# Ten ssm_k blocks in the head with their writes behind the gathers, four logit products of a chunk together, list columns on GpSimd

## The chip, the cores and the metric

One core of one Trainium2 chip runs the whole program in one launch. The metric is device time in microseconds (us): the median of several executions of the program. One more execution was taken by the hardware profiler, and everything said of engines, waits and transfers comes from it.

## What is computed

The reference mixes two branches over 2048 tokens of 512 channels with a gate per token:

```python
x = A_q
g = _sigmoid((x * gate_w).sum(-1, keepdims=True))
a = _A_ref(x, A_k, A_v, A_shift_k, A_ssm_k, A_ssm_D)   # short conv of k, times v, long causal conv with ssm_k, times q
b = _B_ref(x, B_w_router, B_w_gate, B_w_up, B_w_down)  # top 2 of 8 experts: silu(x Wg) * (x Wu) Wd
return g * a + (1 - g) * b
```

`_A_ref` convolves 2048 steps per channel by FFT; `ssm_k` is its kernel. `_B_ref` routes each token to the two experts with the highest logits. Everything is float32, and the kernel keeps that accuracy: a product of the experts is three products of rounded parts (high by high, high by low, low by high).

## The kernel before

**The two branches.** The long convolution is done as a transform in two stages by matrix products. Stage 1 takes 16 blocks of `ssm_k` (here "ks blocks", `k_out` and `stage1_f32`, lines 276 to 314): a block of 128 x 512 is loaded (`kr`), two products with a constant matrix `c1` give 2 x 128 x 512 results, they are copied out of PSUM (`out1`) and written to a scratch `kd` in HBM. 16 blocks of the other input follow (`x_stage1`), then stage 2, the inverse, and `y_stage`. These steps are generators in a list `fill` (line 430), and `tick()` puts one more of them between the tiles of the experts. The experts run one after the other (`expert(r)`, lines 503 to 672): expert `r` has eleven tiles `ft` of the hidden width, with `up(ft)` (products `g` and `u` in two halves of the rows) and a `down` for each group of tiles. So TensorE has one long stream: products of the experts with a ks block, or a step of the other kind, between them now and then.

**The head.** Before the first expert can run, its rows must be known. The head (lines 694 to 934) is written in the order in which each engine is to run it, and kept so (`manual_schedule`); after it the framework orders the rest. It goes like this:

- SyncE loads the transposed input `qT` as 16 tiles `xt` of 128 x 512, four for each of four chunks of 512 tokens, then the constants and the first ks blocks.
- For each chunk (lines 772 to 780), four logit products (line 777) fill four groups of 32 partitions of one PSUM tile. `turn` transposes what an earlier chunk gave, between the second and the third product of the next one, and `ranks` (lines 760 to 767) makes masks of the top two on VectorE, five operations on 128 x 256 per chunk.
- A scan over the masks (line 791) and two pairs of small products (lines 794, 795) count and place the tokens. `key` (line 806) holds the counts; the expert with the most tokens becomes expert 0, its number goes into `eor0` for SyncE and ScalarE, and its rows are listed: `hots` (line 894) is a table of 128 x 16 x 128 zeros and ones in four operations, `vals` its columns (lines 881, 882), the list comes out of 16 products (line 897), and `gidx` (line 869) holds the row numbers.
- Five indirect DMAs on GpSimd (line 460) gather the rows of expert 0. Each gathered tile of 128 rows is transposed on TensorE (line 469, tile `xgp`), and copied out twice: ScalarE writes the rounded part `xh` (line 471), VectorE the rest `xl` (line 472). The first product of expert 0 (`product`, line 555, `hi_first`) takes four steps with `xh`, four with the low part of the weights, then four with `xl` of the first two tiles. `raw` is a tile of gate and up weights, split by ScalarE into `gh` and by VectorE into `gl`.
- Six ks blocks (`SEQ_N`) run in the head. Their results are written to `kd` by SyncE as each copy is done, the sixth by ScalarE after the gathers (`later`). `busy` puts products without a use into gaps of TensorE.

**Buffers.** A ks block's two copies go into two tiles with the tag "A" (six buffers) or one double tile with the tag "ev" (three buffers, `EV`, line 42). The loads `kr` use double tiles with the tag "B" (five). A new tile of a tag takes the buffer of the oldest, and whoever writes it waits until that one was read.

Of the kernel before, what the change touches and what calls it, by code (L numbers as in the profile page):

```python
# [21 lines left out]
P = 128  # L22
# [27 lines left out]
XT = 16  # L50
# [6 lines left out]
SEQ_N = 6  # L57
BUSY = (14, 3, 4, 1, 10, 6, 6)
# [77 lines left out]
def gated_mix(ctx: ExitStack, tc: tile.TileContext, a, out):  # L136
# [113 lines left out]
    def out1(p, dst, pl, name, later=False):  # L250
# [25 lines left out]
    def stage1_f32(x, dst, pl, name, later=False):  # L276
        if ordered and pl % 2 == 0:
            p = [turned(f"{name}p{t}") for t in range(2)]
# [11 lines left out]
        out1(p if ordered else both, dst, pl, name, later)  # L290
# [22 lines left out]
    def k_out(pl, later=False):  # L313
        stage1_f32(kr[pl], kd, pl, f"ks{pl}", later)
# [138 lines left out]
    def load_rows(r, n):  # L453
        w = min(P, CAPS[r] - n * P)
        col = r * TILES + n
        if r == 0 and n >= XG:
            xg = t2k("A", 6, f"xg{r}_{n}")
# [37 lines left out]
    def ticks(n):  # L495
        for _ in range(n):
            tick()

# [4 lines left out]
    def expert(r):  # L503
# [12 lines left out]
        def load(ft, eng=sync):  # L516
            fw = FT[ft][1]
            raw = wp.tile([P, 2 * KT * P], F32, tag="raw", bufs=R3[0], name=f"raw{r}_{ft}")
            n = 2 * KT * fw
            src = a["wgu"][ds(st["e"], 1), GU_OFF[ft]:GU_OFF[ft] + P * n].rearrange("o (p n) -> (o p) n", p=P)  # L520
            if r == 0 and ft in QN and not ordered:
                with after("act 0"):
                    act.dma_start(raw[:, :n], src)
# [4 lines left out]
            st["raw", ft] = raw[:, :n]  # L528

# [13 lines left out]
        def product(ft, h, u, hi_first=False):  # L543
# [13 lines left out]
            for kt in range(KT):  # L557
                last = mm3(p[:fw, :nn], ghv[:, u, kt], glv[:, u, kt], xh[:, kt, sl], xl[:, kt, sl],
                           start=(kt == 0), stop=(kt == KT - 1))
            return last  # L560

        def load_down(ft, eng=sync):
            f0, fw = FT[ft]
            rd = wp.tile([P, D], F32, tag="rd", bufs=R3[3], name=f"rd{r}_{ft}")
            src = a["wd"][ds(st["e"], 1), f0:f0 + fw, :].rearrange("o f d -> (o f) d")
            if r == 0 and ft in QR and not ordered:
                with after("act 0"):
                    act.dma_start(rd[:fw], src)
# [124 lines left out]

    first = expert(0)
# [4 lines left out]
    gt = rp.tile([P, PL * D // S, E, E], F32, name="gt")  # L699
    run = rp.tile([P, E + 1, PL], BF16, name="run")  # L700
    dve.memset(run[:, 0], 0.0)
    NB = S // D
    sums = rp.tile([P, 4, P], BF16, name="sums")
    pool.memset(sums[:, 2], 1.0)
    pool.memset(sums[:, 3], -1.0)
    xts = []
    for c in range(NB):
        for kt in range(KT):
            xts.append(rp.tile([P, D], F32, tag="xt", bufs=XT, name=f"xt{c}_{kt}"))
            anchor["sp"] = sync.dma_start(xts[-1], a["qT"][c, kt]).ins  # L710
        if c == 0:
            sync.dma_start(ident, a["c_small"][:, :P])
# [16 lines left out]
    def keep(c):  # L729
        lgT.append(rp.tile([P, D], F32, tag="lgT", bufs=4, name=f"lgT{c}"))  # L730
        act.activation(lgT[c], lgp[c], AF.Copy)
# [12 lines left out]
    CP = PL // NB  # L744
# [15 lines left out]
    def ranks(c):  # L760
        part = slice(c * CP, c * CP + CP)
        s4 = [P, CP, E, E]
        dve.tensor_reduce(L9[:, part], lt[c].rearrange("p (a k e) -> p a e k", a=CP, k=KT)[:, :, :E + 1], op=ALU.add, axis=AX.X)
        dve.tensor_tensor(gt, L[:, part].unsqueeze(2).to_broadcast(s4), L[:, part].unsqueeze(3).to_broadcast(s4), op=ALU.subtract)
        dve.tensor_tensor(gt, gt, tie.unsqueeze(1).to_broadcast(s4), op=ALU.is_ge)
        dve.tensor_reduce(rank[:, part], gt, op=ALU.add, axis=AX.X)
# [5 lines left out]
    for c in range(NB):  # L772
        for kt in range(KT):
            if c and kt == 2:
                turn(c - 1)
                ranks(c - 1)
            pe.matmul(lgp[c][32 * kt:32 * kt + 32], wk[:, kt], xts[c * KT + kt], start=True, stop=True)
# [4 lines left out]
    turn(NB - 1)  # L782
    ranks(NB - 1)
# [3 lines left out]
    k_out(k_order[0])  # L787
    k_load(k_order[5])
    k_out(k_order[1])
# [7 lines left out]
    k_out(k_order[2])  # L797
    k_out(k_order[3])
# [14 lines left out]
    dve.tensor_tensor(oh0, key, top.to_broadcast([P, E]), op=ALU.is_equal)  # L813
    s0 = rp.tile([P, PL], F32, name="s0")
    n0 = rp.tile([P, PL], F32, name="n0")
    u0 = rp.tile([P, PL], F32, name="u0")
    e0 = rp.tile([P, E], F32, name="e0")
    ef0 = rp.tile([P, 1], F32, name="ef0")
    g5 = rp.tile([P, PL, TILES], F32, name="g5")
    dve.tensor_mul(w0, w0, oh0.unsqueeze(2).to_broadcast([P, E, PL]))  # L820
    dve.tensor_mul(e0, oh0, io8)
    dve.tensor_reduce(s0, w0.rearrange("p e a -> p a e"), op=ALU.add, axis=AX.X)
    dve.tensor_reduce(ef0, e0, op=ALU.add, axis=AX.X)
    s5 = [P, PL, TILES]
# [6 lines left out]
    dve.tensor_tensor(g5, n0.unsqueeze(2).to_broadcast(s5), cols1[:, :TILES].unsqueeze(1).to_broadcast(s5), op=ALU.is_equal)  # L831

# [48 lines left out]
    dve.tensor_scalar(val0[:, :, 1], g5, own, None, op0=ALU.mult)  # L881
    dve.tensor_mul(val0[:, :, 0], g5, tok_hi.unsqueeze(2).to_broadcast(s5))
# [6 lines left out]
    k_out(k_order[4])  # L889
    act.activation(G, L9[:, :, E], AF.Exp, scale=-1.0)  # L890
    first.split(0, act)
    busy(none, BUSY[2])
    for i in range(0, PL, 4):
        dve.tensor_tensor(hot[:, i:i + 4], u0[:, i:i + 4].unsqueeze(2).to_broadcast([P, 4, P]),
                          io128n.unsqueeze(1).to_broadcast([P, 4, P]), op=ALU.is_equal)
        for j in range(i, i + 4):
            pe.matmul(pv0, hot[:, j], val0[:, j], start=(j == 0), stop=(j == PL - 1))
        if i + 4 < PL:
            busy(none, BUSY[3])
    read(0, pv0)  # L900
    k_out(k_order[5], later=True)
# [7 lines left out]
    act.activation(z, z, AF.Exp)  # L909
    rows0 = gather(0)  # L910
    next(rows0)
    busy(none, BUSY[4])
    next(rows0)
    first.split(0, dve, halves=(0,))
    busy(none, BUSY[5])
    next(rows0)
    first.split(0, dve, halves=(1,))
    for f in written:
        f()
    first.load(2, act)  # L920
    first.load_down(0, act)
    act.activation(sg0, key[:, :1], AF.Silu)
    busy(none, BUSY[6])
    first.product(0, 0, 0, hi_first=True)
    next(rows0)
    first.split(1, act)
    anchor["pe"] = first.product(0, 0, 1).ins
# [3 lines left out]
    ordered = False  # L931
    for _ in rows0:
        pass
    ticks(2)
# [234 lines left out]
```

## Time and profile before

| | |
|---|---|
| median of 3 runs | 965.4 us (963.39 to 966.9) |
| the profiled execution: its time | 962.82 us |
| its span | 960.9 us |
| TensorE (PE) busy | 941.3 us, 98% |
| VectorE (DVE), ScalarE (ACT), GpSimd (POOL) busy | 64%, 56%, 15% |
| granted TensorE clock, mean | 0.993 |

A profile is read from what TensorE waits for: with 98% of the span busy, only its few idle stretches and the work in its stream can give time back. A timeline row is one instruction, or several of a kind in a row, with its start, its busy time and, in brackets, the idle time ahead of it with what ended that. Consecutive products overlap, so what one costs in a full stream is the distance between starts.

### The profile page before, as it was taken

How to read it: one execution, taken by the hardware profiler on the slowest of the kernel's cores; microseconds unless marked ns; L12 is line 12 of the kernel's file. 1: busy time of each engine (PE TensorE's matmuls, PEld its weight loads, DVE VectorE, ACT ScalarE, POOL GpSimd, SP SyncE). 2: the span in 40 equal slices, each digit the busy share in tenths (PEclk: the TensorE clock that was granted, in tenths of full speed). 3: DMA queues.
4: the chain of work that ended last, by engine and by line, in shares of the span. 5: the costliest groups of instructions: out<-in, count | busy, mean ns of one | idle time of the engine just before them, and what ended most of it. 6: DMA issues, size and time to landing. Idle time of an engine off the chain costs nothing. (4 is left out here: it accounts for less than half of the span.)

```text
span 960.9 us, 18311 instructions
## 1 busy us (share of the span) xinstructions
PE 941.3 (98%) x7079; PEld 832.4 (87%) x7079; DVE 619.4 (64%) x1160; ACT 538.2 (56%) x881; POOL 139.6 (15%) x125
## 2 busy tenths in 40 slices
PE   8799999999999999999999999999999999999996
PEld 3589999999999999888889898888888887888895
DVE  4597689889999454745656555664676655554541
ACT  3453344454646645678667877677776672334330
POOL 1202011300103020031100301003120301020002
PEclk9899999999999999999999999999999999999998
DMA  8875875644657445474434754457453849875413
GB/s 299 308 265 195 302 244 179 174 149 168 220 179 197 145 135 187 146 183 167 143 129 161 179 170 152 128 169 182 164 165 113 207 143 315 268 197 143 116 31 44
DMA packets 78827, 171.93 MB, mean 179 GB/s; under 512 B 8625, under 2 KB 9521, under 8 KB 78610
## 3 DMA queue, kind: packets, MB, share of 16 engines
q1 hardware_dynamic: 55330, 122.57, 38.7%
q0 software_dynamic: 10976, 23.78, 12.1%
q10 hardware_dynamic: 12432, 24.38, 6.8%
q8 instruction: 57, 0.93, 0.4%
q14 instruction: 32, 0.26, 0.1%
HBM read 127.13 MB, written 43.57 MB: 178 GB/s over the span
## 5 line engine op out<-in xcount | busy, mean ns | idle before, releaser
L197 PE MATMUL g<-xh,gh 128*128 128x256 f32 (+15 forms) x700 | 202.7, 290 | 1.0 <-DVE sg L589 1.0
L197 PE MATMUL u<-xh,gh 128*128 128x256 f32 (+14 forms) x704 | 202.0, 287 | 0.7 <-ACT sg L588 0.6
L198 PE MATMUL u<-xl,gh 128*128 128x256 f32 (+14 forms) x704 | 201.6, 286 | 0.0
L199 PE MATMUL u<-xh,gl 128*128 128x256 f32 (+14 forms) x704 | 201.3, 286 | 0.0
L198 PE MATMUL g<-xl,gh 128*128 128x256 f32 (+15 forms) x700 | 200.1, 286 | 0.0
L199 PE MATMUL g<-xh,gl 128*128 128x256 f32 (+15 forms) x700 | 200.1, 286 | 0.0
L197 PEld LDWEIGHTS g<-xh,gh 128*128 128x128 f32 (+1 forms) x700 | 130.2, 186 | 16.9 <-issue 9.6
L197 PEld LDWEIGHTS u<-xh,gh 128*128 128x128 f32 (+1 forms) x704 | 130.9, 186 | 7.4 <-issue 4.0
L589 DVE TENSOR_TENSOR sg<-sg,u 128x256 f32<-128x256 f32 (+14 forms) x176 | 74.7, 425 | 95.8 <-PE u L199 84.9
L199 PEld LDWEIGHTS u<-xh,gl 128*128 128x128 f32 (+1 forms) x704 | 131.0, 186 | 5.7 <-issue 5.7
L590 ACT ACTIVATE hh<-sg 128x256 fp32r<-128x256 f32 (+14 forms) x176 | 73.5, 419 | 111.2 <-DVE sg L589 110.9
L198 PEld LDWEIGHTS u<-xl,gh 128*128 128x128 f32 (+1 forms) x704 | 131.0, 186 | 5.3 <-issue 4.9
L199 PEld LDWEIGHTS g<-xh,gl 128*128 128x128 f32 (+1 forms) x700 | 130.3, 186 | 5.9 <-issue 5.7
L198 PEld LDWEIGHTS g<-xl,gh 128*128 128x128 f32 (+1 forms) x700 | 130.2, 186 | 5.0 <-issue 3.2
L197 PE MATMUL yp<-hh,dh 128*128 128x264 f32 (+12 forms) x440 | 127.2, 291 | 0.0
L198 PE MATMUL yp<-hl,dh 128*128 128x264 f32 (+12 forms) x440 | 126.6, 289 | 0.0
L199 PE MATMUL yp<-hh,dl 128*128 128x264 f32 (+12 forms) x440 | 126.4, 289 | 0.0
L541 DVE TENSOR_TENSOR gl<-raw,gh 128x1024 fp32r<-128x1024 f32 (+2 forms) x89 | 105.4, 1184 | 22.9 <-ACT gh L535 22.2
L535 ACT ACTIVATE gh<-raw 128x1024 fp32r<-128x1024 f32 (+1 forms) x88 | 91.2, 1036 | 42.4 <-PE u L198 31.1
L588 ACT ACTIVATE sg<-g 128x256 f32<-128x256 f32 (+14 forms) x176 | 67.4, 386 | 80.8 <-PE g L199 72.2
L597 ACT ACTIVATE dh<-rd 128x512 fp32r<-128x512 f32 (+1 forms) x88 | 53.3, 627 | 70.5 <-DMA rd<-in_wd 30.6
L460 POOL DMA_INDIRECT xg<-in_q,gidx x37 | 44.7, 1207 | 325.8 <-PE xgp L469 288.7
(286 smaller groups left out, 1614.3 us busy)
## 6 DMA issues: line engine op xcount, KB each, us to landing
raw<-in_wgu SPq DMA_DIRECT2D x78, 512.0 KB
rd<-in_wd SPq DMA_DIRECT2D x77, 256.0 KB
kl<-kd SPq DMA_DIRECT2D x16, 512.0 KB
xl<-xd SPq DMA_DIRECT2D x32, 256.0 KB
zd<-ze ACTq DMA_DIRECT2D x16, 512.0 KB
zl<-zd SPq DMA_DIRECT2D x16, 512.0 KB
out<-zt SPq DMA_DIRECT2D x21, 256.0 KB
krow<-in_kpad SPq DMA_DIRECT2D x19, 256.0 KB
```

What stands on the lines that cost most here:

```text
L197: pe.matmul(p, wh, hi, start=start, stop=False)
L198: pe.matmul(p, wh, lo, start=False, stop=False)
L199: return pe.matmul(p, wl, hi, start=False, stop=stop)
L460: anchor["pool"] = pool.indirect_dma_start(out=xg[:w], out_offset=None, in_=a["q"], in_offset=bass.IndirectOffsetOnAxis(ap=gidx[:w, col:co ...
L535: act.activation(st["gh", ft], raw, AF.Copy)
L541: dve.tensor_sub(st["gl", ft][:, c], raw[:, c], st["gh", ft][:, c].bitcast(F32))
L588: act.activation(sg[:fw, :nn], pp[0][:fw, :nn], AF.Silu)
L589: dve.tensor_mul(sg[:fw, :nn], sg[:fw, :nn], pp[1][:fw, :nn])
L590: act.activation(hh[:fw, sl], sg[:fw, :nn], AF.Copy)
L597: act.activation(dh[:fw], rd[:fw], AF.Copy)
```

## The change

- **Logits.** The fifth entry of `NCH` splits the last chunk into two halves of 256 tokens; each half comes in one DMA whose rows are 256 elements long. The four logit products of a chunk stand together, and `turn` and `ranks` of the chunk before come ahead of them.
- **ks blocks.** Ten of them (`SEQ_N`) run in the head; all ten are loaded ahead of the expert's weights. All their writes to `kd` become `later`, that is, they are issued by GpSimd behind the gathers. Blocks 7, 8 and 10 are copied out by VectorE, 9 by ScalarE, 7 and 9 into "B" tiles, all other even ones into "ev" tiles. The two `tick()` at the end of the head are gone, and `c2` is loaded later.
- **The list.** `e0`, its sum and `eor0` move from VectorE to GpSimd, and so do the two list columns; the comparison that gave `g5` becomes a difference of neighbours in a wider comparison (`g6`). `hots` is made from `u0` and a table `io4`, both bf16, with four neighbours innermost, and its four operations feed 16 products that stand without `busy` between them. `xg` tiles 3 and 4 use "xt" buffers, of which there are now 12.
- **Counts.** `BUSY` has new numbers.

```diff
-XT = 16
+XT = 12
-SEQ_N = 6
-BUSY = (14, 3, 4, 1, 10, 6, 6)
+SEQ_N = 10
+BUSY = (14, 3, 1, 6, 3)
...
-        if pl % 2:
+        both = None
+        if home == "A":
             evs = [t2k("A", 6, f"{name}e{t}") for t in range(2)]
         else:
-            both = two("ev", f"{name}e")
+            both = two(home, f"{name}e")
             evs = [half(both, t) for t in range(2)]
         for t in range(2):
-            act.activation(evs[t], p[t], AF.Copy)
-            if later:
-                written.append(lambda t=t: act.dma_start(dst[:, t, pl, :], evs[t]))
+            if eng is dve:
+                dve.tensor_copy(evs[t], p[t])
             else:
+                act.activation(evs[t], p[t], AF.Copy)
+            if not later:
                 sync.dma_start(dst[:, t, pl, :], evs[t])
+        if later and both is not None:
+            written.append(lambda: pool.dma_start(dst[:, :, pl, :], split2(both)))
+        elif later:
+            written.extend(lambda t=t: pool.dma_start(dst[:, t, pl, :], evs[t]) for t in range(2))
...
+NCH = (4, 4, 4, 2, 2)
...
+            x2 = rp.tile([P, KT, n], F32, tag="x2", bufs=2, name=f"xt{c}")
+            anchor["sp"] = sync.dma_start(x2, a["qT"][b].rearrange("k p d -> p k d")[:, :, o:o + n]).ins
...
     for c in range(NB):
         for kt in range(KT):
-            if c and kt == 2:
-                turn(c - 1)
-                ranks(c - 1)
...
         busy(lgp[-1], BUSY[1])
+        turn(c)
+        ranks(c)
...
+    pool.tensor_mul(e0, oh0, io8)
...
+    for h in (4, 2, 1):
+        pool.tensor_add(e0[:, :h], e0[:, :h], e0[:, h:2 * h])
+    pool.tensor_copy(eor0, e0[:, :1])
...
+    pool.tensor_sub(g5, g6[:, :, :TILES], g6[:, :, 1:])
...
-    dve.tensor_scalar(val0[:, :, 1], g5, own, None, op0=ALU.mult)
-    dve.tensor_mul(val0[:, :, 0], g5, tok_hi.unsqueeze(2).to_broadcast(s5))
+    pool.tensor_mul(val0[:, :, 1], g5, own.unsqueeze(2).to_broadcast(s5))
+    pool.tensor_mul(val0[:, :, 0], g5, tok_hi.unsqueeze(2).to_broadcast(s5))
...
+    hot0 = hots[:, :PL * P].rearrange("p (i c j) -> p i c j", i=4, j=4)
+    for i in range(4):
+        dve.tensor_tensor(hot0[:, i], u0[:, 4 * i:4 * i + 4].unsqueeze(1).to_broadcast([P, P, 4]), io4, op=ALU.is_equal)
+        for j in range(4):
+            n = 4 * i + j
+            pe.matmul(pv0, hot0[:, i, :, j], val0[:, n], start=(n == 0), stop=(n == PL - 1))
...
     rows0 = gather(0)
     next(rows0)
+    k_out(k_order[6], home="B", eng=dve, later=True)
+    first.split(0, dve, halves=(0, 1))
+    evict = k_out(k_order[7], home="ev", banks_of=bank, eng=dve, later=True, hold=True)
+    busy(none, BUSY[3])
+    next(rows0)
+    evict()
+    evict = k_out(k_order[8], home="B", later=True, hold=True)
     busy(none, BUSY[4])
     next(rows0)
...
+    evict()
+    evict = k_out(k_order[9], home="ev", banks_of=turned, eng=dve, later=True, hold=True)
+    first.product(0, 0, 0, hi_first=True)
+    first.split(1, act)
+    evict()
     next(rows0)
-    first.split(0, dve, halves=(1,))
+    first.load(2, act)
+    first.load_down(0, act)
     for f in written:
         f()
...
-    ticks(2)
```

Three places of the order that comes out. First VectorE (DVE) around the first gathered tiles; `waits` names the kinds of semaphore an instruction waits on (`DMASW` ones are counted up by DMAs that GpSimd issued, `DMAHW` ones by those of SyncE and ScalarE). Before:

```order
L472 TENSOR_TENSOR xl_407<-xgp_0_428,xh_406 128x4x128 [waits Activation_49]
L541 TENSOR_TENSOR gl_0_435<-raw_0_346,gh_0_360 128x512 [waits DMAHW6_49]
L472 TENSOR_TENSOR xl_407<-xgp_1_443,xh_406 128x4x128 [waits Activation_49]
L541 TENSOR_TENSOR gl_0_435<-raw_0_346,gh_0_360 128x512
L472 TENSOR_TENSOR xl_407<-xgp_2_477,xh_406 128x4x128 [waits Activation_49]
L541 TENSOR_TENSOR gl_1_599<-raw_1_348,gh_1_484 128x1024 [waits DMAHW7_49,Activation_49]
```

and now, from the low part of the first weights on:

```order
L545 TENSOR_TENSOR gl_0_430<-raw_0_359,gh_0_402 128x1024 [waits DMAHW0_49,Activation_49]
L479 TENSOR_TENSOR xl_413<-xgp_0_442,xh_412 128x4x128 [waits Activation_49]
L264 COPY ks8e<-ks8p_432 128x512 [waits DMASW0_49]
L264 COPY ks8e<-ks8p_433 128x512
L479 TENSOR_TENSOR xl_413<-xgp_1_458,xh_412 128x4x128 [waits Activation_49]
L545 TENSOR_TENSOR gl_1_626<-raw_1_361,gh_1_485 128x1024 [waits DMAHW1_49,Activation_49]
L264 COPY ks10e<-ks10p_468 128x512 [waits DMASW3_49,PE_49]
L264 COPY ks10e<-ks10p_469 128x512
L479 TENSOR_TENSOR xl_413<-xgp_2_490,xh_412 128x4x128 [waits Activation_49]
```

The copies of blocks 8 and 10 now stand ahead of `xl` of tiles 1 and 2, and each waits on a DMA of GpSimd. Block 8 takes the buffer "ev" that block 2 had, and block 10 that of block 4, since only three are there (blocks 2, 4, 6, 8, 10 use them in turn); so the two waits are for the writes of blocks 2 and 4 to `kd`.

Second GpSimd (POOL), from the gathers of expert 0 on. Before:

```order
L460 DMA xg_0_408<-in_q,gidx 128x512 [waits DVE_49]
L460 DMA xg_1_410<-in_q,gidx 128x512
L460 DMA xg_2_412<-in_q,gidx 128x512
L460 DMA xg_3_414<-in_q,gidx 128x512 [waits DMAHW5_49,Activation_49]
L460 DMA xg_4_416<-in_q,gidx 56x512 [waits DMAHW6_49,Activation_49]
L311 TENSOR_TENSOR kr_1681<-kr_1681,dD 1x512 [waits DMAHW4_49,DMAHW2_49,DMAHW7_49,DMAHW1_49,PE_49]
```

and now:

```order
L467 DMA xg_0_414<-in_q,gidx 128x512 [waits DVE_49]
L467 DMA xg_1_416<-in_q,gidx 128x512
L467 DMA xg_2_418<-in_q,gidx 128x512
L467 DMA xg_3_420<-in_q,gidx 128x512 [waits PE_49]
L467 DMA xg_4_422<-in_q,gidx 56x512 [waits DMAHW2_49,PE_49]
L272 DMA kd<-ks1e_285 128x512 [waits Activation_49]
L272 DMA kd<-ks1e_286 128x512 [waits Activation_49]
L270 DMA kd<-ks2e 256x1x512 [waits DMASW0_49,Activation_49]
L272 DMA kd<-ks3e_305 128x512 [waits DMASW1_49,Activation_49]
```

All writes of the ten blocks now stand behind the gathers: the four shown here, then nine more, in the order of the blocks from the other half of 3 to 10. A block that went into two "A" tiles (1, 3, 5) has two writes of 128 rows, another one write of 256 rows. The write of block 2 waits on `DMASW0`, a count that gathers raise.

Third TensorE (PE), from the second gathered tile to the third, now (before, six `busy` products stood between `xgp_1` and the first `g`):

```order
L476 MATMUL xgp_1_458<-ident,xg_1_416 128x128 x4
L292 MATMUL ks10p_469<-kr_155,c_90 128x512
L292 MATMUL ks10p_468<-kr_155,c_90 128x512
L559 MATMUL g_0_0_472<-xh_412,gh_0_402 128x256 x4
L559 MATMUL g_0_0_472<-xh_412,gl_0_430 128x256 x4
L559 MATMUL g_0_0_472<-xl_413,gh_0_402 128x256 x4
L476 MATMUL xgp_2_490<-ident,xg_2_418 128x128 x4
```

The third run of `g`, with `xl`, is the one that needs the VectorE rows above; what is behind it waits with it.

## Rows read from the trace of the kernel before

**Rows 1.** The page, part 1: busy time, share of the span and instructions of each engine.

```profile
PE 941.3 (98%) x7079; PEld 832.4 (87%) x7079; DVE 619.4 (64%) x1160; ACT 538.2 (56%) x881; POOL 139.6 (15%) x125
```

**Rows 2.** The waits of TensorE's queue (PE) over the whole span, the longest: engine, line, tile, what it waited for, us in total, times, longest.

```profile
PE xgp L469 <- DMA xg<-in_q,gidx: 5.7, 1, 5.7
```

**Rows 3.** The timeline of PE from 16 to 45 us: start in us, busy us, engine, line, operation, out<-in, shapes, count, and in brackets the idle time before and what ended it.

```profile
16.00 1.05 PE L777 MATMUL lgp<-xt,wr 128*32 128x512 f32 x4
...
19.32 1.02 PE L286 MATMUL ks2p<-kr,c 64*128 64x512 f32 x4
...
35.00 1.08 PE L469 MATMUL xgp<-ident,xg 128*128 128x128 f32 x4 [5.66 <-DMA xg<-in_q,gidx]
...
39.15 0.90 PE L555 MATMUL g<-xh,gh 128*128 128x256 f32 x4
...
40.37 0.64 PE L555 MATMUL g<-xl,gh 128*128 128x256 f32 x4
...
40.84 0.60 PE L469 MATMUL xgp<-ident,xg 128*128 128x128 f32 x4
...
43.49 1.13 PE L286 MATMUL ks7p<-kr,c 64*128 64x512 f32 x4
...
44.55 0.41 PE L197 MATMUL g<-xh,gh 128*128 128x312 f32 x1
```

**Rows 4.** The same view of PE around one ssm_k block in the stream of products (ks8, block 8).

```profile
49.45 0.30 PE L199 MATMUL u<-xh,gl 128*128 128x312 f32 x1
...
49.69 1.13 PE L286 MATMUL ks8p<-kr,c 64*128 64x512 f32 x4
...
50.97 0.28 PE L198 MATMUL u<-xl,gh 128*128 128x256 f32 x1
```

**Rows 5.** The timeline of VectorE (DVE) from 16 to 39 us, same columns.

```profile
16.45 0.59 DVE L764 TENSOR_TENSOR gt<-L 128x256 f32<-128x256 f32 x1
...
18.46 0.31 DVE L763 TENSOR_REDUCE L<-lt 128x36 f32<-128x144 f32 x1 [0.18 <-PE lt L757]
...
18.81 0.42 DVE L764 TENSOR_TENSOR gt<-L 128x256 f32<-128x256 f32 x1
...
20.41 0.42 DVE L791 TENSOR_TENSOR_SCAN run<-ones,mask 128x128 bf16<-128x128 f32 x1
...
21.18 0.17 DVE L806 SCALAR_TENSOR_TENSOR key<-cn_ps,rc 128x8 f32<-128x8 f32 x1 [0.34 <-PE cn_ps L795]
...
22.18 0.16 DVE L821 TENSOR_TENSOR e<-oh,rc 128x8 f32<-128x8 f32 x1
...
22.30 0.37 DVE L822 TENSOR_REDUCE s<-w 128x16 f32<-128x128 f32 x1
...
23.34 0.23 DVE L831 TENSOR_TENSOR g<-n,rc 128x80 f32<-128x80 f32 x1
...
23.94 2.49 DVE L894 TENSOR_TENSOR hots<-u,rc 128x512 bf16<-128x512 f32 x4
...
27.18 0.17 DVE L869 TENSOR_SCALAR gidx<-idf 128x5 int32<-128x5 f32 x1
...
38.88 0.69 DVE L472 TENSOR_TENSOR xl<-xgp,xh 128x512 fp32r<-128x512 f32 x1 [0.84 <-ACT xh L471]
```

**Rows 6.** Groups of DVE's instructions over the whole span, shapes kept apart, columns as in the group view: line, engine, operation, out<-in, shapes, count, busy us, mean ns of one, idle us before them. These multiply two bf16 tables, the second (`pay`) repeated along the innermost axis.

```profile
L850 DVE TENSOR_TENSOR vals<-hots,pay 128x448 bf16<-128x448 bf16 x20 | 12.4, 663 | 0.0
...
L850 DVE TENSOR_TENSOR vals<-hots,pay 128x160 bf16<-128x160 bf16 x3 | 0.9, 338 | 0.0
```

**Rows 7.** The timeline of GpSimd (POOL) from 15 to 34 us, same columns: the first two rows are small operations, the last two the first and the last of the five gathers of expert 0.

```profile
15.92 0.29 POOL L784 CAST sums<-before 128x128 bf16<-128x128 f32 x1 [13.85 <-DMA before<-in_c_small]
...
16.30 0.45 POOL L785 TENSOR_TENSOR before<-before,ident 128x128 f32<-128x128 f32 x1
...
27.63 1.06 POOL L460 DMA_INDIRECT xg<-in_q,gidx  x1 [10.31 <-DVE gidx L869]
...
32.78 0.93 POOL L460 DMA_INDIRECT xg<-in_q,gidx  x1 [0.30 <-issue]
```

**Rows 8.** Groups of POOL's instructions over the whole span: line, engine, operation, out<-in, count, busy us, mean ns of one, idle us before them. `mi` is 128 rows, `ye` to `out` 256 rows of 2 KB.

```profile
L295 POOL DMA_DIRECT2D mi<-in_c_mi x16 | 10.0, 626 | 93.9 <-PE zp L368 68.8 <-PE u L199 14.3 <-PE u L198 10.7
...
L427 POOL DMA_DIRECT2D out<-ye x8 | 9.8, 1225 | 109.5 <-DVE ye L425 103.8 <-DMA out<-ya,sidx 5.7
```

**Rows 9.** Stretches of the span: us from:to, busy us of PE, PEld, DVE, ACT and POOL with instruction counts, granted TensorE clock (1.00 is 2.4 GHz, 0.50 is 1.2 GHz), DMA share, GB/s.

```profile
11.00:12.00 1.00, 1.00 (x9) 0.35 (x7) 0.93 (x3) 0.60 (x1) 0.00 (x0) 1.00 1.05 389
...
14.00:15.00 1.00, 1.00 (x9) 0.35 (x7) 0.93 (x3) 0.60 (x1) 0.00 (x0) 1.00 1.10 361
...
33.00:34.00 1.00, 0.00 (x0) 0.00 (x0) 0.00 (x0) 1.00 (x2) 0.71 (x1) 0.50 1.01 404
...
39.00:40.00 1.00, 1.00 (x8) 0.93 (x7) 1.00 (x2) 0.00 (x0) 0.00 (x0) 0.72 0.86 297
...
75.00:80.00 5.00, 4.73 (x83) 4.62 (x80) 5.00 (x11) 1.64 (x4) 0.00 (x0) 1.00 1.02 373
...
86.00:87.50 1.50, 1.50 (x15) 1.50 (x14) 1.50 (x5) 0.38 (x1) 1.20 (x2) 1.00 0.75 188
```

**Rows 10.** The timeline of SyncE's DMA queue (SPq) after the gathers, same columns as the others.

```profile
38.88 1.51 SPq L221 DMA_DIRECT2D kr<-in_ssk  x3
```

**Rows 11.** The timeline of PE at the second of the later list products.

```profile
77.38 1.24 PE L858 MATMUL list<-vals,hots 128*128 128x70 bf16 x32 [0.27 <-DVE vals L850]
```

More of the change, by code (lines that the diff above doesn't have):

```diff
@@ L247, in gated_mix, with out1 @@
     written = []
-    def out1(p, dst, pl, name, later=False):
+    def out1(p, dst, pl, name, later=False, home=None, eng=None):
         if not ordered:
@@ L273, in stage1, with stage1_f32 @@
         out1(p, dst, pl, name)
-    def stage1_f32(x, dst, pl, name, later=False):
-        if ordered and pl % 2 == 0:
-            p = [turned(f"{name}p{t}") for t in range(2)]
+    def stage1_f32(x, dst, pl, name, later=False, home=None, eng=None, banks_of=None, hold=False):
+        if ordered and banks_of is not None:
+            p = [banks_of(f"{name}p{t}") for t in range(2)]
         else:
@@ L289, in stage1_f32 @@
             first = i
-        out1(p if ordered else both, dst, pl, name, later)
+        evict = lambda: out1(p if ordered else both, dst, pl, name, later, home, eng)
+        return evict if hold else evict()
     def mats(src, i, tag):
@@ L311, in k_load, with k_out @@
             pool.tensor_add(kr[0][0:1, :], kr[0][0:1, :], dD)
-    def k_out(pl, later=False):
-        stage1_f32(kr[pl], kd, pl, f"ks{pl}", later)
+    def k_out(pl, **how):
+        return stage1_f32(kr[pl], kd, pl, f"ks{pl}", **how)
     def k_stage1(pl):
@@ L456, in load_rows @@
         if r == 0 and n >= XG:
-            xg = t2k("A", 6, f"xg{r}_{n}")
+            xg = rp.tile([P, D], F32, tag="xt", bufs=XT, name=f"xg{r}_{n}")
         else:
@@ L559, in product @@
                            start=(kt == 0), stop=(kt == KT - 1))
+            if (r, ft, h, u) == (0, 0, 1, 1):
+                anchor["pe"] = last.ins
             return last
@@ L692, in gated_mix @@
     dve.memset(ones, 1.0)
+    NCH = (4, 4, 4, 2, 2)
+    NB = len(NCH)
+    A0 = [sum(NCH[:c]) for c in range(NB)]
     first = expert(0)
@@ L707, in gated_mix @@
     for c in range(NB):
-        for kt in range(KT):
-            xts.append(rp.tile([P, D], F32, tag="xt", bufs=XT, name=f"xt{c}_{kt}"))
-            anchor["sp"] = sync.dma_start(xts[-1], a["qT"][c, kt]).ins
+        n, b, o = NCH[c] * P, A0[c] // 4, A0[c] % 4 * P
+        if n == D:
+            for kt in range(KT):
+                xts.append(rp.tile([P, D], F32, tag="xt", bufs=XT, name=f"xt{c}_{kt}"))
+                anchor["sp"] = sync.dma_start(xts[-1], a["qT"][b, kt]).ins
+        else:
+            x2 = rp.tile([P, KT, n], F32, tag="x2", bufs=2, name=f"xt{c}")
+            anchor["sp"] = sync.dma_start(x2, a["qT"][b].rearrange("k p d -> p k d")[:, :, o:o + n]).ins
+            xts += [x2[:, kt] for kt in range(KT)]
         if c == 0:
@@ L718, in gated_mix @@
     k_load(k_order[2])
-    sync.dma_start(late, a["c_small"][:, P:NLATE])
     k_load(k_order[3])
     k_load(k_order[4])
+    sync.dma_start(late, a["c_small"][:, P:NLATE])
+    for n in range(5, SEQ_N):
+        k_load(k_order[n])
     with after("sp"):
         pool.dma_start(cr, a["c_r"])
-    sync.dma_start(c2, a["c_r2"])
     lgT, lgp = [], []
     def keep(c):
-        lgT.append(rp.tile([P, D], F32, tag="lgT", bufs=4, name=f"lgT{c}"))
-        act.activation(lgT[c], lgp[c], AF.Copy)
+        lgT.append(rp.tile([P, D], F32, tag="lgT", bufs=4, name=f"lgT{c}")[:, :NCH[c] * P])
+        act.activation(lgT[c], lgp[c][:, :NCH[c] * P], AF.Copy)
     mf0, mf1, mf2 = (fp.tile([P, 2 * P], F32, tag="mf", bufs=3, name=f"r{i}") for i in range(3))
@@ L786, in gated_mix @@
     pool.tensor_mul(sums[:, 1], sums[:, 3], before)
-    k_out(k_order[0])
-    k_load(k_order[5])
-    k_out(k_order[1])
+    pool.tensor_copy(io4, io128n.unsqueeze(2).to_broadcast([P, P, 4]))
+    k_out(k_order[0], home="A", later=True)
+    k_out(k_order[1], home="ev", banks_of=turned, later=True)
     dve.tensor_tensor_scan(run[:, 1:].rearrange("p e a -> p (e a)"), ones, mask.rearrange("p e a -> p (e a)"),
@@ L796, in gated_mix @@
     none = bank("none")
-    k_out(k_order[2])
-    k_out(k_order[3])
+    k_out(k_order[2], home="A", later=True)
+    k_out(k_order[3], home="ev", banks_of=turned, later=True)
     cnt = cn_ps[:, :E]
@@ L888, in gated_mix @@
         first.load(ft)
-    k_out(k_order[4])
+    k_out(k_order[4], home="A", later=True)
     act.activation(G, L9[:, :, E], AF.Exp, scale=-1.0)
-    first.split(0, act)
[L892 to L901, printed above, removed]
+    busy(none, BUSY[2])
+    hot0 = hots[:, :PL * P].rearrange("p (i c j) -> p i c j", i=4, j=4)
[4 more added lines that the diff above has]
+            pe.matmul(pv0, hot0[:, i, :, j], val0[:, n], start=(n == 0), stop=(n == PL - 1))
+    read(0, pv0)
+    k_out(k_order[5], home="ev", banks_of=turned, later=True)
+    first.split(0, act)
     dve.tensor_copy(mi0[:, :E], key)
@@ L909, in gated_mix @@
     act.activation(z, z, AF.Exp)
+    act.activation(sg0, key[:, :1], AF.Silu)
     rows0 = gather(0)
     next(rows0)
+    k_out(k_order[6], home="B", eng=dve, later=True)
[5 more added lines that the diff above has]
+    evict = k_out(k_order[8], home="B", later=True, hold=True)
     busy(none, BUSY[4])
     next(rows0)
-    first.split(0, dve, halves=(0,))
-    busy(none, BUSY[5])
+    evict()
[3 more added lines that the diff above has]
+    evict()
     next(rows0)
-    first.split(0, dve, halves=(1,))
+    first.load(2, act)
+    first.load_down(0, act)
     for f in written:
         f()
[L920 to L927, printed above, removed]
+    first.product(0, 0, 1)
     for _ in range(RM - 3):
```

52 lines of the change are left out of this document (24 added, 28 removed).

## The prediction

> **What bounds the kernel now.** I read the share of busy time first, then TensorE's waits, then its timeline, and only then the engines that it waits for. TensorE (PE) is busy 98% of the span, the next engine 64% [rows 1], so time can only come from PE's idle stretches and from the length of its stream. It has one long wait, 5.7 us for the first gathered rows [rows 2]. The timeline shows the place: idle until 35.00, then transposes and the first products, an ssm_k block (7) at 43.49, and from 44.55 a full stream [rows 3]. The end of the program is therefore (the start of that full stream) + (the work in it), and I price both. What comes ahead of the gathers is a chain: last logits, ranks, scan at 20.41, `key` at 21.18, `hots` at 23.94, `gidx` at 27.18 [rows 5], first gather at 27.63 [rows 7].
>
> I make the sum against the profiled execution, 962.82 us; the median of the runs, 965.4, lies 2.6 above it, and I take the difference over to the median.
>
> **Blocks out of the stream.** Blocks 7 to 10 move into the head. Such a block costs the stream between 1.13 us (its busy time) and 1.28 (49.69 to 50.97, its start to the next product's) [rows 4]; I take 1.23. Block 7 lay ahead of 44.55 already; the other three give 3 x 1.23 = 3.7. Call X the time at which the product that stood at 44.55 starts now. The gain is (44.55 - X) + 3.7.
>
> **The last chunk.** Its rows come in two DMAs, with 256 elements where there were 512. GpSimd's wait for `before`, a small transfer queued behind the inputs, ended at 15.92 [rows 7]; my estimate is that the last input lands at 15.3 now. The inputs moved at 389 GB/s, smaller pieces at 361 [rows 9]; a price between 0.2 and 1.2 us for shorter rows is what the two leave open, and I take 0.4: 15.7. Behind it come four products of 256 columns (half of the 1.05 of four with 512 [rows 3]), a copy of 0.4, a transpose, and ranks on half the elements: 1.2 where the span from 18.46 to 20.41 was 1.95 [rows 5]. That would put the scan at 18.3, but PE runs in order and block 2, at 19.32 before [rows 3], now waits for its load, 18.0 by my estimate, ahead of the counting products. I take `key` at 19.3: 1.9 earlier (bounds 1.2 and 2.4).
>
> **From `key` to the first gather** it took 27.63 - 21.18 = 6.45. Off VectorE go `e` (22.18 to 22.30: 0.12), two more as short, and the last `g` with both list columns (23.34 to 23.94: 0.60) [rows 5]: 0.95 together. GpSimd takes them over, three small operations of at most 0.45 [rows 7], beside `hots`, which covers them with 2.49. If that cover went, up to 1.4 us would stand in the chain; I count 0.2 for two places where one short operation now waits for the one before. `hots` itself I take as it is: 2.49. Elements of 16 bits alone do not shorten such an operation here: 448 pairs of bf16 took 663 ns [rows 6], 512 with f32 inputs 0.62 us apart [rows 5]. The columns that PE now reads lie four apart; no row shows that, and between nothing and one more product's 0.35 I take nothing. So 6.45 - 0.95 + 0.2 = 5.7, and the first gather starts at 25.0, 2.6 earlier (bounds 1.2 and 4.2).
>
> **A new wait.** All writes of blocks now stand behind the five gathers on GpSimd's queue, and VectorE's copy of block 8 needs the buffer of block 2, that is, block 2's write *landed*. Behind this copy on VectorE stands `xl` of the second gathered tile, and for that waits the third run of the first product, with all of PE behind it. The queue: gathers from 27.63 to 33.71, 6.1 [rows 7], with 0.3 for what the transfers ahead of them hold; two writes of 128 rows at 0.63; one of 256 rows at 1.2 [rows 8]. Block 2's write is issued 8.9 us after the first gather starts, at 33.9. What landing costs is bounded by two rows: a gather whose issue ended at 85.4 moved its data from 86.0 to 87.5 [rows 9], 2 us; the first gather of the head ended its issue at 28.69 [rows 7] and let PE go at 35.00 [rows 3], 6.3 us. The second has 404 GB/s of loads beside it [rows 9]. Behind the gathers less is in flight, since SyncE's loads stand behind the copies of gathered tiles, as at 38.88 [rows 10]; so I take 2.7, near the first: **36.6**. Two copies cost at most 0.69 each by `xl` of the same shape [rows 5], 1.3 together, and `xl` 0.7: the third run starts at 38.6, where it was 40.37 [rows 3].
>
> **PE's clock behind that wait.** Before, the clock was 0.50 from soon after PE went idle and still 0.72 from 39 to 40 [rows 9], four us after PE resumed. With a second idle stretch of 2 to 3 us I expect 1.2 GHz again behind it. The third run, a transpose and 12 products took 2.34 us (40.37 to 42.71, with the eight transposes behind them 43.49 [rows 3]); at the half clock they are 0.95, 0.72 and 12 x 0.24, and 0.8 for the eight: 5.3. With 0.5 for the copies that block 7 used to cover, X = 44.4. Bounds: 2.5 less at the full clock.
>
> **The sum:** 0.15 + 3.7 = 3.8 us. Everything won in the list (2.6) is spent again on the wait for block 2's write. 962.8 - 3.8 = 959.0 for the profiled execution, **961.6** for the median. Each us of landing is a us of time. The bytes written to `kd` are as many as before, at another time, and I count nothing for them; SyncE's queue loses 10 short issues that nothing waited for. Block 10 needs block 4's write, issued 2.5 later; it reaches only the tile after, and I count nothing.
>
> **Rivals.**
>
> *Early.* GpSimd's writes find idle DMA engines and land at once (2.0, the low row), and PE keeps its clock over the short gap, or the gather starts before 24. Then X lies 3 to 4 us lower: 957.6 to 958.6. For it speaks that PE has two blocks and `busy` products there; against it, that the clock fell within 4 us of idling before [rows 9]. Chance 0.20.
>
> *Faster list.* The four `hots` operations could run at two elements at a time, since both inputs are now 16-bit and contiguous innermost, where in [rows 6] the second input was a repeated one. By the slope of these rows, (663 - 338) / 288 = 1.13 ns an element, 256 fewer in each of four saves 1.2 us: 960.4. Chance 0.12. The Trainium skill ("VectorE: DVE Perf Modes", section "What auto-detection actually checks") has this rule: all tensors of 16 bits with step 1 double the rate of a two-input operation. No row shows it here; by it the time is this rival's.
>
> *Lock.* A VectorE operation with two SBUF inputs took 0.59 at 16.45, when GpSimd's cast and its 128x128 operation ran beside it [rows 5, 7], and 0.42 alone at 18.81. If GpSimd's columns and `hots` hold each other up so, or one wholly waits for the other, up to 1.0 us enters the chain ahead of the gather: 962.6. Chance 0.06. The Trainium skill ("SBUF — State Buffer", section "Who interferes with whom") says that two such operations exclude each other; the row shows 0.17 of delay, less than a whole operation. By that rule this edit speaks against itself.
>
> *Given back.* Between 75 and 80 VectorE is busy 5.00 of 5.00 us and PE only 4.73 [rows 9], with waits like the 0.27 ahead of the second later list product [rows 11]. VectorE's work there does not shrink; with three blocks gone from PE's stream, PE meets it sooner and waits up to 2 us more: 963.6. Chance 0.15.
>
> *Late, the other side.* Block 2's write waits behind loads as the first gather did, or GpSimd's issue of 256 rows waits for room in its queue. By the sum nothing is gained once X reaches 48.25, which is a landing at 40.4, 6.5 us after issue, just beyond the upper row. From 43.3 on it is slower by 0.3%. What speaks for it: 1 MB of block loads and the weights stand on the other queues; what against: nothing landed that late before. With 8 to 11 us of landing, X is 50 to 53: 967 to 970. Chance 0.12.
>
> **How the numbers follow.** The measurement tells some 0.3%, 2.9 us, from no change, so "faster" begins at 962.5. The forecast has 0.35, its own range 960.5 to 963.8 (landing 1.1 us earlier or 2.2 later); 0.6 of it lies below 962.5. Faster: 0.21 + 0.20 (early) + 0.12 (list) = 0.53. Same: 0.14 + 0.06 (lock) + 0.15 (given back) + 0.02 (the near end of late) = 0.37. Slower: 0.10. For the range I take in early and the faster list together (956.4, and 0.9 for the bounds of the other terms) and the near end of late: 955.5 to 967.
>
> **What would show it.** `key` near 19.3 and the first gather near 25.0; a first PE wait for the gathers ending near 32.3; a second PE wait of 2 to 3 us ahead of the third run of `g`, ended by VectorE's `xl`, with VectorE in turn idle ahead of `ks8e` until a DMA of `kd`; a granted clock of 0.50 around it; no block of 7 to 10 behind the first 312-column product, and that product near 44.4. It is wrong if VectorE does not wait ahead of `ks8e`, if the 312-column product starts outside 41 to 47, or if it starts there and the end does not follow it by 3.7 less: then the stream gave time back.

## The result and the profile after

The changed kernel takes **970.28 us** (median of 6 runs, 969.85 to 973.7) against 964.76 (6 runs, 963.31 to 966.9): slower by 0.64%, ratio 1.0064 with a 95% interval of 1.0046 to 1.0083. The forecast was 961.6, with a range of 955.5 to 967, counted from the 965.4 of the first three runs. The profiled execution took 971.32 us, its span 969.4, against 962.82 and 960.9.

TensorE's waits, the longest of the whole span (columns as in [rows 2]):

```profile
PE g L559 <- DVE xl L479: 10.0, 1, 10.0
PE g L199 <- DVE gl L545: 2.2, 1, 2.2
...
PE xgp L476 <- DMA xg<-in_q,gidx: 1.1, 1, 1.1
```

The wait for gathered rows, 5.7 us before [rows 2], has shrunk to 1.1. In its place stands one of 10.0 for `xl`. The timeline of PE shows the place, and answers to [rows 3]:

```profile
30.18 0.63 PE L476 MATMUL xgp<-ident,xg 128*128 128x128 f32 x4 [1.05 <-DMA xg<-in_q,gidx]
...
34.30 0.64 PE L559 MATMUL g<-xh,gl 128*128 128x256 f32 x4
44.95 1.22 PE L559 MATMUL g<-xl,gh 128*128 128x256 f32 x4 [10.01 <-DVE xl L479]
...
48.83 0.98 PE L476 MATMUL xgp<-ident,xg 128*128 128x128 f32 x8
50.37 0.41 PE L197 MATMUL g<-xh,gh 128*128 128x312 f32 x1 [0.55 <-ACT xh L478]
```

The first rows are there 4.8 us earlier than before, but the third run of `g` starts 4.6 later, and the 312-column product, my X, at 50.37 instead of 44.55. VectorE says what it waited for (answers to [rows 5]):

```profile
15.30 0.31 DVE L781 TENSOR_REDUCE L<-lt 128x36 f32<-128x144 f32 x1 [0.78 <-PE lt L773]
...
17.18 0.22 DVE L781 TENSOR_REDUCE L<-lt 128x18 f32<-128x72 f32 x1
...
18.93 0.22 DVE L781 TENSOR_REDUCE L<-lt 128x18 f32<-128x72 f32 x1
...
21.15 0.17 DVE L821 SCALAR_TENSOR_TENSOR key<-cn_ps,rc 128x8 f32<-128x8 f32 x1 [0.34 <-PE cn_ps L810]
...
23.55 1.69 DVE L908 TENSOR_TENSOR hots<-u,io 128x512 bf16<-128x512 bf16 x4
...
31.48 0.69 DVE L479 TENSOR_TENSOR xl<-xgp,xh 128x512 fp32r<-128x512 f32 x1 [1.03 <-ACT xh L478]
43.01 1.29 DVE L264 COPY ks8e<-ks8p 128x512 f32<-128x512 f32 x2 [10.85 <-DMA kd<-ks2e]
44.22 0.68 DVE L479 TENSOR_TENSOR xl<-xgp,xh 128x512 fp32r<-128x512 f32 x1
```

It stood still for 10.85 us ahead of the copy of block 8, until block 2's write to `kd` had landed. GpSimd had issued that write at 33.78 (answers to [rows 7]):

```profile
26.47 1.10 POOL L467 DMA_INDIRECT xg<-in_q,gidx  x1 [1.86 <-DVE gidx L883]
...
33.78 0.73 POOL L270 DMA_DIRECT2D kd<-ks2e  x1
```

So the write took 9.2 us from the start of its issue to landing. At the same time SyncE issued the loads of blocks 11 to 14, behind the copy of tile 1 (its queue, answers to [rows 10]):

```profile
33.40 0.94 SPq L221 DMA_DIRECT2D kr<-in_ssk  x2
```

The stretches show the granted clock (answers to [rows 9], same columns). It is at 1.2 GHz from 38 until 48, behind the start of PE's wait and through its first products (0.98 from 48 to 50), and once more, in part, late in the list (0.50 from 76 to 78):

```profile
38.00:40.00 2.00, 0.00 (x0) 0.00 (x0) 0.00 (x0) 0.00 (x0) 0.07 (x1) 0.50 0.99 331
...
45.00:46.00 1.00, 1.00 (x5) 1.00 (x6) 1.00 (x2) 0.00 (x0) 1.00 (x2) 0.50 1.07 438
```

```profile
70.00:75.00 5.00, 2.85 (x17) 1.70 (x16) 5.00 (x9) 1.18 (x2) 1.81 (x1) 1.00 0.28 111
75.00:80.00 5.00, 5.00 (x25) 3.94 (x24) 5.00 (x13) 2.28 (x5) 0.00 (x0) 0.66 1.02 270
```

### The profile page after: what moved, and what is told of

The parts are those of the page before. It is cut to its first block, busy times and chain, and to the rows that moved or that the text cites. A ratio compares the mean times of both kernels' runs of the same rounds, so it can differ in the third digit from the quotient of the medians.

```text
span 969.4 us, 18322 instructions
## 1 busy us (share of the span) xinstructions
PE 939.5 (97%) x7071; PEld 832.8 (86%) x7071; DVE 622.9 (64%) x1164; ACT 536.6 (55%) x880; POOL 154.2 (16%) x147
## 5 line engine op out<-in xcount | busy, mean ns | idle before, releaser
L545 DVE TENSOR_TENSOR gl<-raw,gh 128x1024 fp32r<-128x1024 f32 (+1 forms) x88 | 105.2, 1196 | 19.3 <-ACT gh L539 18.3
L598 DVE TENSOR_TENSOR hl<-sg,hh 128x256 fp32r<-128x256 f32 (+14 forms) x176 | 75.0, 428 | 29.5 <-ACT hh L597 26.8
```

The costliest lines, as they stand in the source:

```text
L545: dve.tensor_sub(st["gl", ft][:, c], raw[:, c], st["gh", ft][:, c].bitcast(F32))
L598: dve.tensor_sub(hl[:fw, sl], sg[:fw, :nn], hh[:fw, sl].bitcast(F32))
```

## The experiments

Theory W: the wait of VectorE for block 2's write is what makes the kernel slower. Its rivals: the writes or loads would collide anyway, and the wait only be seen elsewhere; or the stream behind the head has become longer by itself. "X" is again the start of the first 312-column product, and run 2, say, is the run of experiment 2. All ratios are to the kernel before, run on the same chip.

### 1. Other buffers for blocks 8 and 10

```diff
-    evict = k_out(k_order[7], home="ev", banks_of=bank, eng=dve, later=True, hold=True)
+    evict = k_out(k_order[7], home="B", banks_of=bank, eng=dve, later=True, hold=True)
...
-    evict = k_out(k_order[9], home="ev", banks_of=turned, eng=dve, later=True, hold=True)
+    evict = k_out(k_order[9], home="B", banks_of=turned, eng=dve, later=True, hold=True)
```

> Blocks 8 and 10 are copied out into B tiles, so VectorE's copies wait for no write; everything else is as in the changed kernel. Theory W (the wait for block 2's write is what costs): the third run of g starts at 34.5 to 36 where it was 44.95, the 312-column product at 38 to 41 where it was 50.37, the clock stays at 1.00, and the time falls by 9 to 12 us to 958 to 961. Rival S (the stream behind the head has become longer by itself, or the writes now collide with the weights and a new wait of the same size appears): the 312-column product starts early, but the time stays at 965 or more.

Measured: **958.99 us**, ratio 0.9952 (0.9937 to 0.9966), 11.3 below the changed kernel. PE there:

```profile
35.20 0.64 PE L559 MATMUL g<-xl,gh 128*128 128x256 f32 x4
...
40.76 0.41 PE L197 MATMUL g<-xh,gh 128*128 128x312 f32 x1 [2.25 <-ACT xh L478]
```

The writes are as many and stand in the same order behind the gathers; the copy no longer waits for one. W holds: X moved by 9.6 us, the time by 11.3. One thing moved besides: with two more "B" buffers taken, SyncE's second load (blocks 13 and 14) went out at 53.03 and no longer beside the first and the writes. One miss: the granted clock did fall, to 0.50 from 42 to 44, behind the 2.25 us for `xh`.

### 2. Loads of blocks 11 to 14 later

```diff
-        if (r, n) == (0, 1):
+        if (r, n) == (0, QA):
             anchor["act 1"] = i.ins
```

> The loads of blocks 11 to 14 (1 MB) are issued behind the copy of gathered tile 2 instead of tile 1, so they are not in flight while block 2's write is. Theory L (the loads share the DMA engines with the writes): block 2's write lands at 37 to 39 where it landed at 43.0, the third run of g starts at 39 to 41, the time is 964 to 967. Theory Q (GpSimd's own queue is what is slow, five gathers and the writes of block 1 ahead): it lands at 41 to 43 and the time is 969 to 971.

Measured: 968.6 us (1.0054; 1.0035 to 1.0072). The landing is as theory L says; in the timeline of VectorE:

```profile
37.72 1.29 DVE L264 COPY ks8e<-ks8p 128x512 f32<-128x512 f32 x2 [5.82 <-DMA kd<-ks2e]
```

The write took 4.2 us from issue to landing instead of 9.2. The queues from 34 to 40 us show why (queue, packets, MB, share of the 16 engines). In the changed kernel, q1 carrying the loads and q0 GpSimd's writes:

```profile
q1 hardware_dynamic: 460, 0.90, 57.5%
q0 software_dynamic: 209, 0.68, 30.9%
```

and in this run:

```profile
q0 software_dynamic: 600, 2.08, 96.5%
```

Over these 6 us the loads took over half of the engines' time, and GpSimd's queue moved a third of the bytes that it moves alone. Sharing is not the whole of it: from 34.6 to 36.6 the engines of the changed kernel moved 134 GB/s in all and were 64% busy, where run 2 has 358 GB/s and 97%. Why they were not full is not shown by any run. X came 4.3 earlier, at 46.08, but the time was 968.6 where I had expected 964 to 967 (the profiled execution took 966.86). Behind X the down weights come late (ScalarE waits 5.5 us for `rd`), and PE waits 3.1 us for `sg`. The four block loads now go out at 42.40, together with those of the weights; as I read it, the collision moved there, which no further run checks.

### 3. Block 2's write first in the queue

```diff
-    for f in written:
+    for f in [written[i] for i in (2, 5, 0, 1, 3, 4)] + written[6:]:
         f()
```

> The writes of blocks 2 and 4 stand directly behind the gathers, ahead of those of 1, 3 and 5; everything else is as in the changed kernel. Theory W with theory L: block 2's write is issued 1.2 us earlier and with 0.5 MB less ahead of it, while the loads of blocks 11 to 14 have hardly begun: VectorE's wait ends at 36 to 38.5 instead of 43.0, the third run of g starts at 38 to 40.5, the 312-column product at 43.5 to 46, time 963 to 966. Rival (the landing is late whatever the place in the queue, because GpSimd's queue is served slowly while loads run): wait ends at 41 or later, time 968 to 970.

Measured: 962.81 us (0.9991; 0.9976 to 1.0006), within the expectation. VectorE and PE:

```profile
37.61 1.29 DVE L264 COPY ks8e<-ks8p 128x512 f32<-128x512 f32 x2 [5.38 <-DMA kd<-ks2e]
```

```profile
45.73 0.41 PE L197 MATMUL g<-xh,gh 128*128 128x312 f32 x1 [0.61 <-ACT xh L478]
```

With the loads of blocks 11 to 14 in place as in the changed kernel, two writes of 0.5 MB moved ahead in a queue were worth 7.5 us, 4.6 of them in X and the rest behind it. The write landed 5.0 us after the start of its issue at 32.65. So the late landing took two things together: a place behind block 1's writes, and loads that began before the write's own turn came. Without either one it is 4 to 5 us instead of 9.2; a run without both was not made.

### 4. The writes at once, from SyncE

```diff
-    k_out(k_order[0], home="A", later=True)
+    k_out(k_order[0], home="A", later=False)
...
```

and so for all ten blocks.

> Each block's results are written to kd by SyncE as soon as they are copied (two DMAs of 128 rows a block), and none by GpSimd; everything else is as in the changed kernel. Theory W: no wait of VectorE for block 2's write; the first weights come behind up to 2 MB of writes and land 3 us later than at 28.1; third run of g at 36 to 39, the 312-column product at 40 to 43, time 960 to 964. Rival C (the writes ahead of the gathers cost the gathers and the weights as much as they save): first gathered rows at 35 or later, time 967 or more.

Measured: 961.19 us (0.9978; 0.9966 to 0.9989). PE:

```profile
31.30 0.63 PE L476 MATMUL xgp<-ident,xg 128*128 128x128 f32 x4 [2.33 <-DMA xg<-in_q,gidx]
...
44.41 0.41 PE L197 MATMUL g<-xh,gh 128*128 128x312 f32 x1 [1.07 <-ACT xh L478]
```

The head is no shorter than before the change (X 44.41 against 44.55 [rows 3]; I had expected 40 to 43), since weights and gathers come behind the writes. The time is 3.1 us lower all the same. With X as before, this is what moving the three blocks out of the stream is worth, near my 3.7: from X to the end of the span PE is busy for 902.15 us, where it was 905.74.

### 5. The last chunk whole

```diff
-XT = 12
+XT = 16
...
-    NCH = (4, 4, 4, 2, 2)
+    NCH = (4, 4, 4, 4)
```

> The last chunk of 512 tokens is one again, loaded as four tiles of 128x512; everything else is as in the changed kernel. Theory V (two halves cost VectorE 1.75 + 1.45 us of ranks where a whole one costs 1.95, so the split wins nothing): key at 20.9 to 21.5 as with the split (21.15), time 969.5 to 971. Theory of the prediction (the split brings key forward by 1 to 2 us and something else takes it back): key at 22.2 to 23.2, time 971 to 972.

Measured: 970.95 us (1.0081; 1.0054 to 1.0107), no difference to the changed kernel that this tells. VectorE:

```profile
18.07 0.31 DVE L781 TENSOR_REDUCE L<-lt 128x36 f32<-128x144 f32 x1 [0.55 <-PE lt L773]
...
20.78 0.17 DVE L821 SCALAR_TENSOR_TENSOR key<-cn_ps,rc 128x8 f32<-128x8 f32 x1 [0.34 <-PE cn_ps L810]
```

`key` is there 0.37 us earlier *without* the split, just under theory V's span of 20.9 to 21.5 and far from 22.2. Its place alone would not tell this, since it lies between 20.92 and 21.69 in the eight runs with the split. But counted from the start of the ranks of the third chunk, `key` comes after 5.84 to 5.86 us in all eight (15.30 to 21.15 in the changed kernel), and after 5.44 without it (15.34 to 20.78; 5.47 in the run below). The same with the other buffers:

> As the run with the other buffers (958.99), with the last chunk whole. Theory V (the two halves cost VectorE what they save): key 0.2 to 0.5 us earlier than with the split, time 957.5 to 959.5. Theory of the prediction (the split brings key forward by 1 to 2 us): time 960 to 961.

Measured: **957.92 us** (0.9939; 0.9925 to 0.9952), X at 39.80, `key` at 20.84. This is the lowest median here and below both kernels; its interval overlaps that of run 1, so a gain over that run is not shown.

### 6. Tables in float32

`u0` and `io4` are float32, one execution.

```diff
-    u0 = rp.tile([P, PL], BF16, name="u0")
+    u0 = rp.tile([P, PL], F32, name="u0")
...
-    io4 = rp.tile([P, P, 4], BF16, name="io4")
+    io4 = rp.tile([P, P, 4], F32, name="io4")
```

> u0 and io4, the inputs of the four hots operations, are float32 instead of bf16, in the same layout; everything else is as in the changed kernel. If the 16-bit inputs are what made hots shorter (1.69 against 2.49): 2.4 to 2.6 us for the four. If the layout alone did: 1.6 to 1.8.

```profile
23.87 2.75 DVE L908 TENSOR_TENSOR hots<-u,io 128x512 bf16<-128x512 f32 x4
```

2.75 us, with 972.74 for that execution: the 16-bit inputs made `hots` shorter, not the layout. It is a little over the span expected, and 0.26 over the 2.49 of before [rows 5], where GpSimd had no columns to make beside it; whether these are the reason was not tried.

### 7. Two attempts on the wait for `xh`

In the run with the other buffers, ScalarE is late with `xh` of tiles 3 and 4 because it is busy issuing weight loads. First these loads stand behind the copies:

```diff
-    first.load(2, act)
-    first.load_down(0, act)
     for f in written:
         f()
     first.product(0, 0, 1)
     for _ in range(RM - 3):
         next(rows0, None)
+    first.load(2, act)
+    first.load_down(0, act)
```

> As the run with the other buffers (958.99), and ScalarE issues the loads of the third weight tile and of the first down tile behind its copies of gathered tiles 3 and 4 instead of ahead of them. Theory I (in that run the 312-column product at 40.76 waits 2.25 us for xh because ScalarE is held by the issue of these loads, 36.5 to 39.8, and the idle time also halves the clock from 41.8 to 44.5): the wait goes, the product starts at 38 to 39, the clock stays at 1.00, time 955 to 957. Rival N (the rows of tiles 3 and 4 or the weights are late next): the product starts as early, but PE waits for the third weight tile or the list later, and the time stays at 958 to 960.

Measured: 964.87 us (1.0001; 0.999 to 1.0011), 5.9 *above* the run without this edit, though X came 0.9 earlier, at 39.83. Theory I fell as a forecast of the time. From 57 to 73 us, in this run:

```profile
57.00:65.00 8.00, 5.41 (x35) 4.19 (x34) 7.97 (x22) 3.10 (x7) 0.00 (x0) 1.00 0.77 273
65.00:73.00 8.00, 6.43 (x42) 4.66 (x40) 8.00 (x16) 4.67 (x8) 0.00 (x0) 1.00 0.82 267
```

and with the other buffers alone:

```profile
57.00:65.00 8.00, 6.60 (x42) 5.25 (x41) 8.00 (x14) 3.85 (x7) 0.00 (x0) 1.00 0.73 268
65.00:73.00 8.00, 8.00 (x54) 6.40 (x52) 8.00 (x16) 3.99 (x7) 1.95 (x1) 1.00 0.98 350
```

VectorE is full in both; PE is busy for 2.8 us less. The later weights are split later (49.31 instead of 47.97 on VectorE) and meet the list's work there. But the order of the instructions behind the head changed with this edit as well, and of PE's waits in these 16 us, 4.15 against 1.40, one of 1.56 is for the load of block 15. Right behind X it waits 1.76 for `sg`, while ScalarE issues the loads that were moved (from 39.47 on). So how much of the 5.9 us is the weights' alone stays open. To tell, SyncE issued these loads early:

```diff
-    first.load(2, act)
-    first.load_down(0, act)
+    first.load(2)
+    first.load_down(0)
```

> As the run with the other buffers (958.99), and SyncE instead of ScalarE issues the loads of the third weight tile and the first down tile, directly behind the first two weight tiles, so ahead of the gathers. Theory G (what counts behind the head is when VectorE can split the third weights, as the run with these loads behind the rows showed: 0.9 us earlier start, 5.9 us longer): the third weights are split several us earlier, ScalarE is free for the copies of tiles 3 and 4, the 312-column product starts at 39 to 40.5, time 955 to 958. Rival C (0.75 MB of loads ahead of the gathers delay them by 1 to 2 us and with them the start): first gathered rows at 31.5 or later, 312-column product at 41 or later, time 959 to 962.

Measured: 963.76 us (1.0; 0.9988 to 1.0011). The rival's mechanism, and more of it than expected: PE waited 3.8 us for the gathered rows, until 33.02, and X was 44.33. So it did not settle the question of the weights.

## Why the prediction was wrong

**The step that failed** is the landing of block 2's write: "so I take 2.7, near the first". What stands around it came as described: VectorE stood ahead of `ks8e`, PE ahead of the third run of `g`, the granted clock was 0.50, and from the third run to X it took 5.4 us (5.8 forecast). The sum has the issue of the write ended at 33.9, and it ended at 34.5. That these are so near is in part luck, since the first gather started 1.5 us later than forecast (26.47, not 25.0) and the queue behind it took 8.0 us instead of 8.9. From 34.5 the write took 8.5 us, not 2.7, beyond even the upper row of 6.3. Both rows were of gathers, neither of a write with others ahead of it.

My reason for the low value was that "less is in flight, since SyncE's loads stand behind the copies of gathered tiles". They do stand there; but the copy of tile 1 ends at 33.4, so those loads start together with the writes and not after them, and block 1's 0.5 MB stands ahead. Runs 2 and 3 show that taking away either one frees 4 to 5 us of landing; run 2, without the loads, still has 3.5 from the end of the issue. The rival "late" named the place and the mechanism, and its X of 50 to 53 held; I gave it a chance of only 0.12. By the sum nothing was to be slower by 0.3% before a landing at 43.3, that is an X of 51.15, which was not quite reached: the rest is below.

**The last chunk** was to bring `key` 1.9 us earlier and brought nothing (21.15 against 21.18). I priced the ranks of the second half, 1.2, and forgot that VectorE does those of the first half just ahead: from 17.18 to 18.93 the one, then the other to 20.38, 3.2 in all where a whole chunk took 1.95. Of the first half's 1.75, 0.3 is more than the second's 1.45: two of its operations took 0.45 and 0.58 beside GpSimd's, and 0.29 each in the second. That is the rival "lock" in a place where I had not looked for it; no edit tried it. PE's wait for block 2's load, which I set as the limit, was not it. Run 5 shows the split to cost 0.4 in this chain.

**From `key` to the first gather** it took 5.32 us, not 5.7: `hots` took 1.69 instead of 2.49 (the rival "faster list", confirmed by run 6), and the short operations left on VectorE took 0.4 more than I counted (2.40 from `key` to `hots`, 2.76 before). The Trainium skill ("VectorE: DVE Perf Modes", section "What auto-detection actually checks") has a rule for `hots`: an operation with two inputs runs at twice the rate if every tensor has 16-bit elements with step 1. The trace agrees in direction: 1.69 against 2.75 for the same four operations.

**The gathered rows** came 3.7 us after the first gather started, where it had been 7.4 [rows 3, 7]; I had carried over the old span. Why they came so much sooner was not tried; from 28 to 30 us all queues together moved 305 GB/s, where in the kernel before it was 405 from 32 to 34. PE had work until 34.9. None of it counted, since the write's landing came last.

**The three blocks** were to save 3.7 us in the stream. Run 4 shows 3.1 at an unchanged X, and 3.6 in PE's busy time behind it. In the changed kernel little of it is left: from X to the end of the span it takes 919.0 us, where it was 916.4 before; with 3.7 less it would be 912.7, so 6.4 were given back. PE is busy for 904.1 us there, 1.7 less than before, and idle for 14.9 (10.6 before), 2.15 of it in one piece:

```profile
74.18 0.39 PE L199 MATMUL g<-xh,gl 128*128 128x256 f32 x1 [2.15 <-DVE gl L545]
```

VectorE, full there, had four big operations of the list and one held small one ahead of that `gl`:

```profile
66.53 4.62 DVE L1036 TENSOR_TENSOR hots<-row,rc 128x1024 bf16<-128x1024 f32 x4
71.08 1.29 DVE L1022 TENSOR_TENSOR s<-s,pay 128x32 f32<-128x32 f32 x1
...
72.91 1.21 DVE L545 TENSOR_TENSOR gl<-raw,gh 128x1024 fp32r<-128x1024 f32 x1
```

and the granted clock fell behind it. That is the rival "given back", near the place that it named, as a second cost and not instead of the first, and larger than the 2 us that I gave it. By the medians: 964.8 + 5.8 (X) - 3.7 = 966.9, and 3.4 of giving back make 970.3; the other 3.0 of the 6.4 are the distances of the two profiled executions from their medians. That VectorE's order there costs this much is read from the profile and was not tried by an edit. From X to the end it takes 914.3 us in run 4, 915.6 in run 3, 916.9 in run 1, 916.4 in the same with the chunk whole, and 923.7 in the first attempt of run 7. None reaches 912.7: what the head wins is never passed on whole.

## What to carry to other kernels

When a change puts writes behind other transfers, look up which buffer's reuse waits for each write and which engine's queue that wait heads; then price the landing with everything that is released at the same moment, not with what was in flight before. A landing can be tested cheaply by another buffer or another place in the queue, and here the two were worth 11.3 and 7.5 us of time. A start that comes earlier pays only as far as the next full engine keeps up: read the time from the end of the head to the end of the program as a number of its own.

## What the runs showed of the hardware

- Loads of SyncE and writes of GpSimd beside each other can move less than the writes alone: from 34 to 40 us the loads had 0.90 MB and GpSimd's queue 0.68, in sum 264 GB/s, where in run 2 that queue alone moved 2.08 MB at 346 GB/s. The shares are not fixed: in run 3, with the writes in another order, the same stretch had 0.77 MB of loads and 1.16 of writes, 322 GB/s.
- A small VectorE operation takes longer beside GpSimd: the 32-element operation at 71.08 took 1.29 us, where the like took 0.19 in the kernel before; GpSimd ran an addition on 1x512 from 70.51 for 1.81 us. In the head an operation on 128x128 took 0.58 at 17.92, beside GpSimd's copy of 128x512 (17.68, 0.68 us), and 0.29 half a chunk later. The Trainium skill ("SBUF — State Buffer", section "Who interferes with whom") lets a VectorE operation with two inputs in SBUF and a GpSimd operation that reads SBUF exclude each other. Both pairs here agree in kind: the first ended with GpSimd's addition (72.37 and 72.32), and the second lost 0.29 us, less than a whole operation. No edit tried either.
